# Columns in five chunks of 512 and one of 452, in a Fourier and two-layer kernel

## The chip, the cores and the metric

The kernel runs on one core of a Trainium2 chip. The metric is device time in microseconds (us) of one execution. The kernel before took 933.95 us as the median of three runs (933.7 to 934.25). Beside these, one execution was recorded by the hardware profiler, and every row below is from it.

## The reference

The input `x` has 2 sequences of 3008 rows with 256 values. A two-dimensional Fourier transform is taken of each sequence, and its real part goes through two layers with their own weights.

```
X = np.fft.fft(np.fft.fft(x, axis=1), axis=2)
x = X.real.reshape(6016, 256)                        # float32
h = x @ w_in;  x = (h / (1 + exp(-h))) @ w_out       # 256 -> 2048 -> 256
h = x @ w_in2; g = h * clip(h + 3, 0, 6) / 6
out = g @ w_out2                                      # 6016 x 256
```

The weights are given in a wide (64-bit) format, which the kernel decodes to 32-bit floats itself.

## The kernel before

The Fourier stage writes a tile `eo` (128 partitions, two halves, one column per pair of rows k and -k). There are 2 x 1505 = 3010 such columns (`NPAIR`), and one column stands for two of the 6016 rows: the even and the odd part of the first layer's product, added and subtracted, give both.

All later work goes by chunks of columns, the list `CHUNKS` (line 54). With `CHUNK = 502` there are five chunks of 502 columns and one of 500. A chunk of n columns gives matmuls with n moving columns, and vector instructions of n columns. Tiles with moving data (`x..`, `h`, `ghi`, `glo`) are allocated with 512 columns per half (`LINE`) and used up to n; the staging tiles `st` and `u` and the DRAM buffers follow `CHUNK` or n.

Every 32-bit matrix product is done as three matmuls, helper `mm3` at lines 301 to 303: both operands are split into a high and a low part, and high x high, high x low and low x high are added up in PSUM. Each of these matmuls loads its own 128 x 128 weights.

**First layer** (lines 551 to 660, driven by the loop over `units`). A unit is one chunk and one of 16 blocks of 128 hidden values. `win1` and `win1_end` make the even and the odd product (tile `ab`, 2 x 3 matmuls); VectorE adds the last input row (line 559) and combines them (line 570); `parts` computes the activation on ScalarE; `low` makes the low parts on GpSimd, and for every other unit one of the two on VectorE (line 621); `wout1` makes four products into `y` (4 x 3 matmuls). So a unit has 18 matmuls. The chunks are passed twice: a first pass over 2, 4, 4, 6, 8 and 10 blocks (`PARTS`), a second over the rest. The second pass's result is added to the first's in DRAM by an accumulating store that GpSimd issues (line 663). Beside these units VectorE decodes the weights of both layers; `advance(steps, PACE + ...)` gives the decoder a fixed number of nanoseconds per unit, whatever the width of the chunk.

**Second layer** (the loop over `units2`). A unit is one chunk and two hidden blocks. The 2 x 2 block product is made with seven products instead of eight (tiles `pa`, `pb`, `pc`, `pd`, 7 x 3 matmuls), and `wout2` makes eight products into `y` (8 x 3): 45 matmuls, and 8 units per chunk. The last chunk comes last in both layers' order of chunks.

The order of the work on each engine is written out in the program. SyncE issues the plain transfers; ScalarE issues a few at the start and the end. Dynamic transfers, those of GpSimd, have a scratch area of 16 KB of each SBUF partition, at its start; the program's own tiles lie behind it.

Of the kernel before, what the change touches and what calls it, by code (L numbers as in the profile page):

```python
# [36 lines left out]
F32 = mybir.dt.float32  # L37
# [7 lines left out]
S, D, B = 3008, 256, 2  # L45
NA, NB = 47, 64
NPAIR = B * (S // 2 + 1)
SELF = NB // 2 + 1
HALFB = NPAIR // B
FF, P = 2048, 128  # L50
NF = FF // P
CHUNK = 502
LINE = 512
CHUNKS = [(c, min(CHUNK, NPAIR - c)) for c in range(0, NPAIR, CHUNK)]


NJ = NB // 4
# [24 lines left out]
def body(tc, xh, x128, t1, t2, t3, w1, w128, w2, out):  # L82
    nc = tc.nc
    V, A, T, G = nc.vector, nc.scalar, nc.tensor, nc.gpsimd
# [4 lines left out]
    eop = tc.alloc_tile_pool(name="eop", bufs=1, side="right")  # L89
# [1 line left out]
    w128_sb = per.tile([P, NF], F32, name="w128_sb")  # L91
    consts = per.tile([P, 16], F32, name="consts")
    three, mask, minus, warm = (consts[:, i : i + 1] for i in range(4))
    eo = eop.tile([P, 2, NPAIR], F32, name="eo", tag="eo")
    w2_d = [
        [dr.tile([P, 2, n], F32, name=f"w2{q}_d{g}", tag=f"w2{q}_d{g}") for q, n in (("h", 512), ("l", 512), ("x", 384))]
        for g in range(NF // 2)
    ]
    e128_d = [dr.tile([1, n], F32, name=f"e128_d{j}", tag=f"e128_d{j}") for j, (_, n) in enumerate(CHUNKS)]
    x_d = [[dr.tile([P, 2, n], F32, name=f"x{h}_d{j}", tag=f"x{h}_d{j}") for h in "hl"] for j, (_, n) in enumerate(CHUNKS)]  # L100
    y1_d = [dr.tile([P, 2, 2 * n], F32, name=f"y1_d{j}", tag=f"y1_d{j}") for j, (_, n) in enumerate(CHUNKS)]

# [321 lines left out]
        return c + 256  # L424

    V.memset(three, 3.0)
    G.memset(nil, 0.0)
    cleared = (V, ((2, 0, 1), (2, 2, 3), (3, 0, 2))), (G, ((2, 1, 2), (2, 3, 4), (3, 2, 4), (4, 0, 4), (5, 0, 4)))
    for eng, slots in cleared:
# [17 lines left out]
    i = g = 0  # L447
# [56 lines left out]
    def split_eo(k, j):  # L504
        c, n = CHUNKS[j]
        hi, lo = (xsp.tile([P, 2, LINE], F32R, name=f"x{h}{k}", tag=f"x{2 * (k % 2) + i}") for i, h in enumerate(("hi", "lo")))
        eb = xsp.tile([P, LINE], F32, name=f"eb{k}", tag="eb", bufs=2)
        new = k < len(CHUNKS)
        if new:
            nc.sync.dma_start(e128_d[j], eo[0:1, 1, c : c + n])  # L510
        nc.sync.dma_start(eb[:, :n], e128_d[j].to_broadcast([P, n]))
        if new:
            split(hi[:, :, :n], lo[:, :, :n], eo[:, :, c : c + n], x_d[j])
        else:
            for x, d in zip((hi, lo), x_d[j]):
                nc.sync.dma_start(x[:, :, :n].bitcast(F32), d)
        return hi, lo, eb
# [3 lines left out]
    units = [(k, f) for k, (_, fs) in enumerate(segs) for f in fs]  # L521
    n1 = NF * len(CHUNKS)
    turn = n1 - 10
# [87 lines left out]
    stp = tc.alloc_tile_pool(name="stp", bufs=1, reuse_waits="tile")  # L611
# [15 lines left out]
    def stage_tile(i):  # L627
        return stp.tile([P, 2, 2 * CHUNK], F32, name=f"st{i}", tag=f"st{i}")

# [38 lines left out]
    def moving(k):  # L668

        j = segs2[k][0]
        n = CHUNKS[j][1]
        st = stp.tile([P, 4 * CHUNK + 8], F32, name=f"u{k}", tag="su", bufs=1)
        st = st[:, : 4 * CHUNK].rearrange("p (m c) -> p m c", m=2)
        nc.sync.dma_start(st[:, :, : 2 * n], y1_d[j])
        b11, b12 = st[:, 0, 0:n], st[:, 0, n : 2 * n]
        b21, b22 = st[:, 1, 0:n], st[:, 1, n : 2 * n]
        us[k] = {}

        def high(name, src):
            r = ring[0] % RING
            ring[0] += 1
            x = (xsp if r < NEAR else xq).tile([P, 2, LINE], F32R, name=f"{name}_{k}", tag=f"x{r}")
            us[k][name] = x[:, 0, :n], x[:, 1, :n]
            A.activation(x[:, 0, :n], src, AF.Copy)

        def rest(name, src):
            hi, lo = us[k][name]
            (V if k == 0 and name in ("b21", "t2", "t3") else G).tensor_tensor(out=lo, in0=src, in1=hi, op=ALU.subtract)  # L690

        yield
        high("b11", b11)
        yield
        rest("b11", b11)
        high("b21", b21)
        yield
        rest("b21", b21)
        yield
        V.tensor_tensor(out=b11, in0=b12, in1=b11, op=ALU.subtract)  # L700
        V.tensor_tensor(out=b12, in0=b22, in1=b12, op=ALU.subtract)
        high("t1", b11)
        yield
        rest("t1", b11)
        yield
        V.tensor_tensor(out=b11, in0=b22, in1=b11, op=ALU.subtract)
        V.tensor_tensor(out=b21, in0=b11, in1=b21, op=ALU.subtract)
        high("t2", b11)
        yield
        rest("t2", b11)  # L710
        high("t4", b21)
        yield
        rest("t4", b21)
        high("t3", b12)
        yield
        rest("t3", b12)
        high("b22", b22)
        yield
        rest("b22", b22)
        yield  # L720
# [25 lines left out]
    for i in range(n1):  # L746
        k, f = units[i]
# [34 lines left out]
        if i == n1 - 15:  # L782
            ready = moving(0)
            next(ready)
# [89 lines left out]
    for e, (k, f) in enumerate(units2):  # L874
        j, fs = segs2[k]
        n = CHUNKS[j][1]
        u = us[k]
# [37 lines left out]
        if left == 3 and more:  # L915
            ready = moving(k + 1)
            next(ready)
# [114 lines left out]
def token_columns():  # L1032

    at = {(k % NA, k % NB): k for k in range(S)}
    ks = [at[ka, kb] for ka in range(NA // 2 + 1) for kb in range(NB if ka else SELF)]
    pairs = [(n, k) for n in range(B) for k in ks]
    col = np.zeros(B * S, np.int64)
    for c, n in CHUNKS:
        for i in range(n):
            m, k = pairs[c + i]  # L1040
            col[m * S + (S - k) % S] = 2 * c + n + i
            col[m * S + k] = 2 * c + i
    return col
# [44 lines left out]
```

## Time and profile before

| | |
|---|---|
| median of three runs | 933.95 us (933.7 to 934.25) |
| the profiled execution | 934.05 us, span 932.3 us |
| TensorE busy | 926.3 us (99%), 4286 matmuls |
| VectorE, ScalarE, GpSimd busy | 659.5, 651.8, 530.8 us |
| granted TensorE clock, mean | 0.999 |

The span runs from the first to the last instruction of the profiled execution. A matmul's row has its start and a length; matmuls overlap (the next one starts before the one before has ended), so what counts for the time is the distance between two starts. Weight loads have rows of their own (PEld) and run beside the matmuls. "128x502" in a row is partitions x columns.

### The profile page before, as it was taken

What the parts mean: (1) busy time and instruction counts of PE and PEld (TensorE: products, weight loads), DVE (VectorE), ACT (ScalarE), POOL (GpSimd) and SP (SyncE); (2) the same over time, 40 slices, a digit from 0 to 9 for tenths busy, and PEclk for the clock granted to TensorE, in tenths of its full rate; (3) what the DMA queues carried; (4) which work ended last, traced back from release to release, by engine and by line L of the source; (5) the groups of instructions that cost most, each with busy time, mean ns of one, the idle gap of its engine ahead of it and who ended that gap; (6) DMA issues with size and microseconds to landing.
All of it is one profiled execution on the core that took longest, in us unless ns stands there. A gap on an engine that the chain in (4) does not pass through costs nothing.

```text
span 932.3 us, 12162 instructions
## 1 busy us (share of the span) xinstructions
PE 926.3 (99%) x4286; PEld 775.2 (83%) x4286; DVE 659.5 (71%) x907; ACT 651.8 (70%) x1144; POOL 530.8 (57%) x391
## 2 busy tenths in 40 slices
PE   9999999999999999999999999999999999999998
PEld 8988888888888888888888888888888888888886
DVE  7988898979999999865564565564554555455544
ACT  4878767675767676857776777766776677677665
POOL 2056656654656656534774577755765675576553
PEclk9999999999999999999999999999999999999999
DMA  8554334052273636586130002020020002001001
GB/s 322 196 200 155 135 145 145 1 190 98 101 222 115 200 118 196 176 296 213 63 88 1 1 1 89 0 89 1 1 89 0 1 1 89 1 0 45 1 1 44
DMA packets 27720, 89.27 MB, mean 96 GB/s; under 512 B 2886, under 2 KB 16460, under 8 KB 25132
## 3 DMA queue, kind: packets, MB, share of 16 engines
q1 hardware_dynamic: 26284, 81.81, 24.4%
q0 software_dynamic: 992, 6.16, 3.6%
q8 instruction: 33, 0.54, 0.2%
q10 hardware_dynamic: 384, 0.54, 0.2%
q14 instruction: 27, 0.22, 0.1%
HBM read 52.30 MB, written 36.20 MB: 95 GB/s over the span
## 4 chain that ended last, share of the span: by engine, by line
PE 98%; DMA 0%; DVE 0%; issue 0%; ACT 0%; SPq 0%; DVEq 0%
PE y L301 19%; PE y L302 18%; PE y L303 18%; PE ab L301 5%; PE ab L302 5%; PE ab L303 5%; PE pa L301 4%; PE pa L302 4%; PE pa L303 3%; PE pb L302 2%; PE pb L301 2%; PE pb L303 2%; PE ps L366 1%; PE ps L409 1%; PE pd L302 1%; PE pd L301 1%
## 5 line engine op out<-in xcount | busy, mean ns | idle before, releaser
L805 POOL TENSOR_TENSOR glo<-h,ghi 128x502 fp32r<-128x502 f32 (+1 forms) x191 | 246.6, 1303 | 195.0 <-ACT ghi L802 195.0
L621 POOL TENSOR_TENSOR glo<-h,ghi 128x502 fp32r<-128x502 f32 (+1 forms) x137 | 219.2, 1615 | 188.8 <-ACT h L580 183.1
L301 PE MATMUL y<-ghi,whi 128*128 128x502 f32 (+1 forms) x768 | 298.0, 388 | 0.0
L302 PE MATMUL y<-glo,whi 128*128 128x502 f32 (+1 forms) x768 | 298.0, 388 | 0.0
L303 PE MATMUL y<-ghi,wlo 128*128 128x502 f32 (+1 forms) x768 | 297.8, 388 | 0.0
L303 PEld LDWEIGHTS y<-ghi,wlo 128*128 128x128 f32 x768 | 144.2, 188 | 29.3
L301 PEld LDWEIGHTS y<-ghi,whi 128*128 128x128 f32 x768 | 144.2, 188 | 29.0
L302 PEld LDWEIGHTS y<-glo,whi 128*128 128x128 f32 x768 | 144.2, 188 | 28.9
L802 ACT ACTIVATE ghi<-h 128x502 fp32r<-128x502 f32 (+1 forms) x192 | 118.1, 624 | 47.1 <-DVE h L797 46.8
L579 ACT ACTIVATE ghi<-ab 128x502 fp32r<-128x502 f32 (+1 forms) x96 | 56.5, 588 | 88.5 <-DVE h L570 87.5
L797 DVE SCALAR_TENSOR_TENSOR h<-h,pc 128x502 f32<-128x502 f32 (+1 forms) x96 | 65.1, 678 | 71.7 <-ACT h L794 71.7
L927 DVE TENSOR_TENSOR pc<-u,pb 128x502 f32<-128x502 f32 (+1 forms) x48 | 32.9, 685 | 111.7 <-ACT u L863 111.7
L863 ACT ACTIVATE u<-pa 128x502 f32<-128x502 f32 (+1 forms) x96 | 56.7, 591 | 54.9 <-PE pa L303 52.0
L794 ACT ACTIVATE h<-pc,consts 128x502 f32<-128x502 f32 (+1 forms) x96 | 64.6, 673 | 40.1 <-DVE pc L927 39.0
L559 DVE SCALAR_TENSOR_TENSOR st<-eb,w_sb,ab 128x502 f32<-128x502 f32 (+1 forms) x92 | 67.0, 728 | 19.0 <-PE ab L303 19.0
L301 PE MATMUL ab<-xhi,whi 128*128 128x502 f32 (+1 forms) x192 | 75.2, 392 | 0.1
L302 PE MATMUL ab<-xlo,whi 128*128 128x502 f32 (+1 forms) x192 | 74.7, 389 | 0.0
L303 PE MATMUL ab<-xhi,wlo 128*128 128x502 f32 (+1 forms) x192 | 74.5, 388 | 0.0
L570 DVE SCALAR_TENSOR_TENSOR h<-st,ab 128x502 f32<-128x502 f32 (+1 forms) x92 | 61.4, 668 | 7.0 <-PE ab L303 6.3
L797 DVE SCALAR_TENSOR_TENSOR h<-h,pd 128x502 f32<-128x502 f32 (+1 forms) x96 | 64.5, 671 | 1.2 <-ACT h L794 1.2
L794 ACT ACTIVATE h<-pd,consts 128x502 f32<-128x502 f32 (+1 forms) x96 | 64.7, 674 | 0.6 <-DVE pd L939 0.6
L580 ACT ACTIVATE h<-h 128x502 f32<-128x502 f32 (+1 forms) x96 | 60.0, 625 | 3.0
(165 smaller groups left out, 1572.2 us busy)
## 6 DMA issues: line engine op xcount, KB each, us to landing
raw<-in_w SPq DMA_DIRECT2D x16, 1024.0 KB, 6.9
u<-y_d SPq DMA_DIRECT2D x6, 1004.0 KB, 6.9
y_d<-st SPq DMA_DIRECT2D x5, 1004.0 KB, 4.4
y_d<-st POOLq DMA_DIRECT2D x5, 1004.0 KB, 9.2
out<-st SPq DMA_DIRECT2D x20, 251.0 KB, 2.3
w2h_d<-h SPq DMA_DIRECT2D x8, 512.0 KB, 2.6
w2l_d<-t SPq DMA_DIRECT2D x8, 512.0 KB, 2.6
whi<-w2h_d SPq DMA_DIRECT2D x8, 512.0 KB, 8.9
```

Source lines behind the costliest of these rows:

```text
L301: T.matmul(o, wh, xhi, start=first, stop=False, **group)
L302: T.matmul(o, wh, xlo, start=False, stop=False, **group)
L303: T.matmul(o, wl, xhi, start=False, stop=last, **group)
L559: V.scalar_tensor_tensor(out=z[:, :n], in0=eb[:, :n], scalar=w128_sb[:, f : f + 1], in1=ab[:, :n], op0=ALU.mult, op1=ALU.add)
L570: V.scalar_tensor_tensor(out=h[:, 0, :n], in0=z[:, :n], scalar=2.0, in1=ab[:, :n], op0=ALU.mult, op1=ALU.subtract)
L580: A.activation(h[:, s, :n], src, AF.Silu)
L621: eng.tensor_tensor(out=glo[:, s, :n], in0=h[:, s, :n], in1=ghi[:, s, :n], op=ALU.subtract)
L794: A.activation(h[:, i, :n], c[:, :n], AF.Relu, bias=three)
L797: V.scalar_tensor_tensor(out=h[:, i, :n], in0=h[:, i, :n], scalar=6.0, in1=c[:, :n], op0=ALU.min, op1=ALU.mult)
L802: A.activation(g[0][:, i, :n], h[:, i, :n], AF.Copy)
L805: E.tensor_tensor(out=g[1][:, i, :n], in0=h[:, i, :n], in1=g[0][:, i, :n], op=ALU.subtract)
L863: A.activation(t[:, :n], pa[:, :n], AF.Copy)
```

## The change

`CHUNK` becomes 512 and a new constant `NCOL` = 3012 takes the place of `NPAIR` where columns are counted: there are five chunks of 512 and one of 452. The tile `eo` and the output have two columns more; the two columns of `eo` are set to zero by a memset on VectorE at the start, and on the host they are dropped from the output. The tile `u` loses 8 elements of padding. The scratch for dynamic transfers is set to 8192 bytes of each partition, so that tiles allocated from that side lie 8 KB lower.

```
-CHUNK = 502
+NCOL = 3012
+CHUNK = 512
-CHUNKS = [(c, min(CHUNK, NPAIR - c)) for c in range(0, NPAIR, CHUNK)]
+CHUNKS = [(c, min(CHUNK, NCOL - c)) for c in range(0, NCOL, CHUNK)]
...
-    eo = eop.tile([P, 2, NPAIR], F32, name="eo", tag="eo")
+    eo = eop.tile([P, 2, NCOL], F32, name="eo", tag="eo")
...
     V.memset(three, 3.0)
+    V.memset(eo[:, :, NPAIR:], 0.0)
...
-        st = stp.tile([P, 4 * CHUNK + 8], F32, name=f"u{k}", tag="su", bufs=1)
+        st = stp.tile([P, 4 * CHUNK], F32, name=f"u{k}", tag="su", bufs=1)
...
-        for i in range(n):
+        for i in range(min(n, NPAIR - c)):
...
-    nc = bacc.Bacc("TRN2", target_bir_lowering=False, num_devices=1)
+    nc = bacc.Bacc("TRN2", target_bir_lowering=False, num_devices=1, dynamic_dma_scratch_size=8192)
...
-    out = nc.dram_tensor("out", (P, 2, 2 * NPAIR), F32, kind="ExternalOutput").ap()
+    out = nc.dram_tensor("out", (P, 2, 2 * NCOL), F32, kind="ExternalOutput").ap()
```

## Rows read from the trace of the kernel before

**Rows 1.** The page: busy us (share) and instructions of each engine; the chain's shares.
```profile
PE 926.3 (99%) x4286; PEld 775.2 (83%) x4286; DVE 659.5 (71%) x907; ACT 651.8 (70%) x1144; POOL 530.8 (57%) x391
...
PE 98%; DMA 0%; DVE 0%; issue 0%; ACT 0%; SPq 0%; DVEq 0%
```
**Rows 2.** The chain of waits, its first long piece: start us, us, what.
```profile
1.19 4.26 DMA x<-in_xh
```
**Rows 3.** Groups by shape, PE: line, names, shapes xcount | busy us, mean ns | idle.
```profile
L301 PE MATMUL y<-ghi,whi 128*128 128x502 f32 x640 | 249.0, 389 | 0.0
L301 PE MATMUL ab<-xhi,whi 128*128 128x502 f32 x160 | 62.9, 393 | 0.1
L301 PE MATMUL pa<-t,whi 128*128 128x502 f32 x40 | 15.8, 395 | 0.0
```
**Rows 4.** Timeline of PE, first layer, 502 columns: start us, us, instruction.
```profile
301.47 0.39 PE L301 MATMUL ab<-xhi,whi 128*128 128x502 f32 x1
305.55 0.39 PE L301 MATMUL ab<-xhi,whi 128*128 128x502 f32 x1
```
**Rows 5.** Timeline of PE, first layer, 500 columns.
```profile
159.30 0.38 PE L301 MATMUL ab<-xhi,whi 128*128 128x500 f32 x1
163.26 0.38 PE L301 MATMUL ab<-xhi,whi 128*128 128x500 f32 x1
```
**Rows 6.** Timeline of PE, second layer, 502 columns.
```profile
707.71 0.39 PE L301 MATMUL pb<-b,wx 128*128 128x502 f32 x1
717.92 0.39 PE L301 MATMUL pb<-b,wx 128*128 128x502 f32 x1
```
**Rows 7.** Timeline of PE, second layer, 500 columns.
```profile
870.51 0.39 PE L301 MATMUL pb<-b,wx 128*128 128x500 f32 x1
875.93 0.38 PE L301 MATMUL pd<-t,whi 128*128 128x500 f32 x1
880.55 0.39 PE L301 MATMUL pb<-b,wx 128*128 128x500 f32 x1
```
**Rows 8.** Windows: stretch, its us, busy us (x) by engine, PEclk, DMA share, GB/s.
```profile
150.00:190.00 40.00, 40.00 (x182) 33.95 (x181) 38.55 (x44) 26.23 (x45) 23.60 (x14) 1.00 0.25 84
210.00:390.00 180.00, 179.89 (x793) 148.46 (x792) 174.58 (x206) 121.45 (x212) 105.53 (x67) 1.00 0.46 146
```
**Rows 9.** Groups by shape, VectorE (columns as in Rows 3).
```profile
L559 DVE SCALAR_TENSOR_TENSOR st<-eb,w_sb,ab 128x502 f32<-128x502 f32 x76 | 55.4, 728 | 12.7 <-PE ab L303 12.7
L570 DVE SCALAR_TENSOR_TENSOR h<-st,ab 128x502 f32<-128x502 f32 x76 | 50.8, 668 | 2.7 <-PE ab L303 2.2 <-issue 0.4
L621 DVE TENSOR_TENSOR glo<-h,ghi 128x502 fp32r<-128x502 f32 x44 | 35.9, 815 | 6.2 <-ACT h L580 6.1
L341 DVE TENSOR_TENSOR x<-x 128x512 f32<-128x512 f32 x4 | 2.8, 692 | 0.3
L341 DVE TENSOR_TENSOR x<-x 128x256 f32<-128x256 f32 x5 | 2.1, 426 | 0.2
L426 DVE MEMSET consts<- 128x1 f32 x1 | 0.1, 59 | 0.8 <-PEq L1076 0.8
```
**Rows 10.** The chain of waits, 310 to 330 us (columns as in Rows 2).
```profile
319.38 0.53 issue
319.90 1.63 DVE a L234
```
**Rows 11.** The page, DMA queues: queue, kind: packets, MB, share of 16 engines.
```profile
q0 software_dynamic: 992, 6.16, 3.6%
```
**Rows 12.** Groups by shape, GpSimd (columns as in Rows 3).
```profile
L663 POOL DMA_DIRECT2D y_d<-st x6 | 5.6, 928 | 0.0
```
**Rows 13.** Groups by shape, weight loads (columns as in Rows 3).
```profile
L301 PEld LDWEIGHTS y<-ghi,whi 128*128 128x128 f32 x768 | 144.2, 188 | 29.0
L409 PEld LDWEIGHTS ps<-t_sb,o 128*128 128x128 f32 x96 | 11.7, 192 | 0.4 <-issue 0.2
```
**Rows 14.** The chain of waits in the Fourier stage (columns as in Rows 2).
```profile
20.36 0.89 PE ps L409 x8
```

More of the change, by code (lines that the diff above doesn't have):

```diff
@@ L1085 @@
     y = np.asarray(r.results[0]["out"])
-    y = y.transpose(2, 1, 0).reshape(2 * NPAIR, D)
+    y = y.transpose(2, 1, 0).reshape(2 * NCOL, D)
     return np.ascontiguousarray(y[token_columns()])
```

## The prediction

> **What bounds the kernel now.** I read the page's busy line first: TensorE is busy 926.3 of 932.3 us, with 4286 matmuls, and nothing else is over 71% [rows 1]. The chain of waits comes next: it is TensorE for 98% of it [rows 1], after a first 4.26 us of input [rows 2]. So the time is the number of matmuls times the distance between their starts, and the question of this change is how that distance depends on the number of moving columns. The groups by shape give the counts [rows 3]. Of the three matmuls of each product there is one group each, so 3 x 640 + 3 x 160 + 21 x 40 = 3240 matmuls have 502 columns; the last chunk has 648 with 500, by the same code (16 units of 18 and 8 of 45). The 389 ns in these rows are not the price of one, since matmuls overlap; the distance of the starts is. The timeline gives it over whole units:
> - first layer, 502 columns: 301.47 to 305.55, one unit of 18 matmuls, 4.08 us, 226.7 ns each [rows 4]
> - first layer, 500 columns: 159.30 to 163.26, 3.96 us, 220.0 ns each [rows 5]
> - second layer, 502 columns: 707.71 to 717.92, one unit of 45, 10.21 us, 226.9 ns [rows 6]
> - second layer, 500 columns: 870.51 to 880.55, 10.04 us, 223.1 ns; in it the 24 matmuls up to 875.93 take 225.8 ns, and the 21 after that 220.0 [rows 7]
>
> The granted clock is 1.00 of 2.4 GHz [rows 8], so streaming alone would be 209.2 ns for 502 columns and 208.3 for 500. The surplus is 17.5 ns (42 columns) for 502 and 11.7 ns (28 columns) for 500. Two columns less save 6.7 ns, where streaming explains 0.8. That is the most telling fact of this profile.
>
> **The change part by part.** The number of matmuls, units and instructions stays as it is (six chunks before and after). Moved are the columns: 10 more in 3240 matmuls, 48 fewer in 648, which is 3240 x 10 - 648 x 48 = 1296 columns more, 0.5 us of streaming. By streaming alone the change is worth nothing; all of it lies in the surplus.
>
> No row has 512 or 452 columns. The bounds for 512: 213.3 ns, streaming with no surplus, and 230.8 ns, with the 42 columns of the 502 row. For 452: 188.3 ns at the low end; at the high end 220.0, if something other than the columns set the 500 row. 500, 512 and 452 are multiples of four, 502 is not; I take the nearest row of that kind, 500, and its 28 columns: 540 cycles, **225.0 ns for 512**, and 480 cycles, **200.0 ns for 452**. The step by step sum:
> - first layer, 512: 18 x 225.0 = 4.05 us for 4.08, 80 units: -2.4 us
> - second layer, 512: 45 x 225.0 = 10.125 for 10.21, 40 units: -3.4
> - first layer, 452: 18 x 200.0 = 3.60 for 3.96, 16 units: -5.8
> - second layer, 452: 45 x 200.0 = 9.00 and the 0.14 that today's 10.04 has over 45 x 220.0; 9.14 for 10.04, 8 units: -7.2
>
> This makes -18.8 us, if TensorE stays the bound. Two things take from it, both on VectorE in the first layer, where it decodes weights at a fixed amount per unit beside its two to three instructions on the chunk (lines 559 and 570, and 621 every other unit) [rows 9]. One column costs it (692 - 426) / 256 = 1.04 ns by line 341 [rows 9]. The last chunk's first pass (10 units) runs in the stretch 150 to 190, where VectorE is busy 38.55 of 40 us [rows 8], 3.82 us per unit of 3.96. With 48 columns fewer in 2.5 instructions it needs 3.82 - 0.125 = 3.69 us, over TensorE's 3.60: +0.9 us over 10 units. In 210 to 390 it has 174.58 of 180 us [rows 8], 3.96 per unit of 4.08; with 10 columns more that is 3.98 of 4.05, so its slack shrinks from 0.12 to 0.07 us. There is one visible stall there now, at 319.38, behind a decode step [rows 10]; I count 0.4 us for more like it.
>
> The other parts I cost at nothing. The zeroed two columns are one small memset on VectorE ahead of the memsets of input buffers; it is hidden by the 4.26 us of the first load [rows 2], and without that cover is under 0.1 us (the memset of one column, line 426, takes 59 ns [rows 9]). The smaller scratch concerns the six accumulating stores of GpSimd, 992 packets in all, 0.93 us of issue each [rows 11, 12]; nothing in the trace shows a limit that half the room would reach, GpSimd's products are short of work (57% busy [rows 1]), and they would hide a wait of several us. Were a store to hold GpSimd until the one before has landed, its cost would be bounded by six waits; stores are tens of us apart, so there is nothing to wait for. Transfers grow by 2%, under matmuls.
>
> Sum: -18.8 + 0.9 + 0.4 = -17.5 us. The profiled execution took 934.05 us with a span of 932.3, 0.1 us over the median of 933.95; so the forecast is 933.95 - 17.5 = **916.5 us**.
>
> Could the weight load hold the short chunk back? It lasts 188 ns, starts with the matmul before, and is nearly as long as 452 columns stream [rows 13, 14]. But in the Fourier stage 8 loads and 8 matmuls go by in 0.89 us, 111 ns a pair, with loads of 192 ns [rows 13, 14], so the duration of a load is latency and not its distance to the next. I keep it as a small rival.
>
> **The rivals.**
> (a) *Groups of sixteen, with a whole 512.* Sixteen columns take 6.67 ns at 2.4 GHz, and both distances are whole multiples: 220.0 is 33, 226.7 is 34. If columns are fetched in sixteens and the ragged end of 502 costs a group more than that of 500, a 512 without a ragged end goes in 33 (220.0 ns) and 452 in 30 (200.0). Second layer: 9.90 + 0.14 = 10.04 for 10.21, 40 x 0.17 = -6.8; first layer: 3.96, but VectorE's 3.98 holds the 44 units of 210 to 390, some -0.09 there and -0.12 in 36 others, -8.3; last chunk -13.0 + 0.9. With 0.6 us of stalls: -26.6, **907 us**. For it speaks the exactness of the multiples; against it that 500 and 502 fill the same 32 groups.
> (b) *Groups of sixteen, rounded up after a constant.* (n + 28) rounded up to sixteen: 500 gives 528 cycles, 502 gives 544, exactly the rows; 512 gives 544 too, 226.7 ns, no gain, and 452 gives 480. Then only the short chunk pays: -13.0 + 0.9 + 0.6 = -11.5, **922 us**. For it: one constant explains both rows; against it: 500 then lies exactly on the edge by chance.
> (c) *The surplus is that of a ragged end and goes.* A whole 512 near 213.3 to 218 ns. At 213.3: second layer 9.60 + 0.14 = 9.74, -18.8; first layer 3.84, held at 3.98 in 44 units, -4.4, and -8.6 in the others; last chunk -12.1: -43.9, **890 us**. For it: streaming is all that 512 columns need; against it: no row of four-byte columns shows a surplus so small. The Trainium skill, "TensorE: Matmul & The Clock Gate", section "Wait — 56ns, not 53.3ns?", states such a rule, that back-to-back matmuls start N / 2.4 GHz and about 2.5 ns apart once warm, 215.7 ns for 512; by it the estimate would be 896 us. The trace differs from that rule in all its rows, by 9 ns for 500 columns and 15 for 502.
> (d) *Slower.* 512 keeps the 42 columns of the 502 row: 230.8 ns. First layer 4.155 for 4.08, 80 units: +6.0; second layer 10.39 for 10.21, 40 units: +7.2; 452 at the same surplus, 205.8 ns: -4.1 and -5.1. Together +4.0, **938 us**. It decides from the point where 512 costs 3.7 ns more than 502 does now (230.4 ns: 3240 x 3.7 = 12.1, the gain of the short chunk). For it: the surplus would be one of the long chunk; against it: two fewer columns already take 6.7 ns off.
> (e) *No gain in the short chunk.* The load of the weights sets 220.0 ns for 500 and for 452: with (b) that is no change, **934 us**. Against it the 111 ns in the Fourier stage.
>
> **How the numbers follow.** Forecast 0.30, (a) 0.27, (b) 0.22, (c) 0.11, (d) 0.06, (e) 0.04. Time 916.5 us. From (a) to (b), with some 5 us to either side for the unknown share of second-layer stretches at the slower distance, and part of (c): 893 to 928 us. A measurement of this kernel can tell about 0.2% (1.9 us) from no change. Faster 0.90 (forecast, a, b, c), same 0.04 (e), slower 0.06 (d).
>
> **What would show it.** In the timeline of the changed kernel the starts of first-layer matmuls of 512 columns stand 225.0 ns apart (a unit of 18 in 4.05 us), those of 452 columns 200.0. 220.0 and 4.0 us would be (a), 226.7 and 4.08 (b), 213 to 218 (c), 230.8 (d); 452 at 220 is (e). In the last chunk's first pass VectorE should be without idle time and the unit near 3.7 us, not 3.6. The forecast is wrong if the distance for 512 is one of the rivals', or if the last chunk's second pass takes other than 9.0 to 9.3 us per unit.

## The result and the profile after

The changed kernel took **943.81 us** (943.47 to 944.09, four runs) against 933.9 of before on the same chip: ratio 1.0106, interval 1.0088 to 1.0123. It is 9.9 us slower; 916.5 was forecast, and the range ended at 928. The profiled execution has a span of 941.7 us, 9.4 more than before.

The page says at once where not to look: TensorE is still busy 99% of the span, with the same 4286 matmuls, and the other engines do what they did [rows 1].

```profile
PE 935.3 (99%) x4286; PEld 773.4 (82%) x4286; DVE 662.6 (70%) x908; ACT 651.2 (69%) x1144; POOL 529.9 (56%) x391
```

So each matmul must have become dearer. The timeline of PE over whole units (start us, us, instruction) shows by how much: first layer with 512 columns (two rows, one unit apart), first layer with 452, second layer with 512, second layer with 452.

```profile
301.73 0.39 PE L302 MATMUL ab<-xhi,whi 128*128 128x512 f32 x1
305.93 0.39 PE L302 MATMUL ab<-xhi,whi 128*128 128x512 f32 x1
...
158.41 0.37 PE L302 MATMUL ab<-xhi,whi 128*128 128x452 f32 x1
162.13 0.37 PE L302 MATMUL ab<-xhi,whi 128*128 128x452 f32 x1
...
709.48 0.39 PE L302 MATMUL pb<-b,wx 128*128 128x512 f32 x1
719.96 0.39 PE L302 MATMUL pb<-b,wx 128*128 128x512 f32 x1
...
875.50 0.37 PE L302 MATMUL pb<-b,wx 128*128 128x452 f32 x1
884.74 0.37 PE L302 MATMUL pb<-b,wx 128*128 128x452 f32 x1
```

The first-layer unit of 18 takes 4.20 us with 512 columns, 233.3 ns a matmul; with 502 it took 4.08 [rows 4]. With 452 it takes 3.72 us, 206.7 ns, for 3.96 with 500 [rows 5]. The second-layer unit of 45 takes 10.48 us for 10.21 [rows 6], and 9.24 for 10.04 [rows 7]. Over 80 and 40 units of the long chunks and 16 and 8 of the short one these four differences account for the time: 80 x 0.12 + 40 x 0.27 = 20.4 us more in the long chunks, 16 x 0.24 + 8 x 0.80 = 10.2 us less in the short one; 10.2 us more together, where the span grew by 9.4.

Over streaming (213.3 and 188.3 ns) the surplus is 20.0 ns, 48 columns, for 512, and 18.4 ns, 44 columns, for 452. The prediction had given both the 28 columns of 500.

VectorE, the second mechanism of the prediction, holds nothing here. These are the windows that answer to [rows 8]:

```profile
150.00:190.00 40.00, 40.00 (x191) 35.57 (x190) 38.06 (x45) 27.16 (x49) 24.00 (x16) 1.00 0.25 86
210.00:390.00 180.00, 180.00 (x773) 144.25 (x772) 173.80 (x203) 118.61 (x203) 105.13 (x66) 1.00 0.43 142
```

TensorE is busy in all of both. The stretch 150 to 190 has 191 matmuls, 10.6 units, most of them of 452 columns (from 176 us on some are of 512 again). VectorE needs 38.06 / 10.6 = 3.59 us a unit there, less than TensorE's 40 / 10.6 = 3.77.

### The profile page after: what moved, and what is told of

Same layout as the page of the kernel before. It is cut to its first block, busy times and chain, and to the rows that moved or that the text cites. A ratio compares the mean times of both kernels' runs of the same rounds, so it can differ in the third digit from the quotient of the medians.

```text
span 941.7 us, 12164 instructions
## 1 busy us (share of the span) xinstructions
PE 935.3 (99%) x4286; PEld 773.4 (82%) x4286; DVE 662.6 (70%) x908; ACT 651.2 (69%) x1144; POOL 529.9 (56%) x391
## 4 chain that ended last, share of the span: by engine, by line
PE 98%; ACT 1%; DVE 0%; DMA 0%; issue 0%; SPq 0%; DVEq 0%
PE y L302 18%; PE y L304 18%; PE y L303 18%; PE ab L302 5%; PE ab L303 5%; PE ab L304 5%; PE pa L303 3%; PE pa L302 3%; PE pa L304 3%; PE pb L302 2%; PE pb L304 2%; PE pb L303 2%; PE ps L367 1%; PE pc L302 1%; PE ps L410 1%; PE pd L303 1%
## 5 line engine op out<-in xcount | busy, mean ns | idle before, releaser
L807 POOL TENSOR_TENSOR glo<-h,ghi 128x512 fp32r<-128x512 f32 (+1 forms) x191 | 246.5, 1303 | 196.3 <-ACT ghi L804 192.6
L623 POOL TENSOR_TENSOR glo<-h,ghi 128x512 fp32r<-128x512 f32 (+1 forms) x137 | 216.0, 1593 | 198.3 <-ACT h L582 188.8
L302 PE MATMUL y<-ghi,whi 128*128 128x512 f32 (+1 forms) x768 | 299.5, 390 | 0.0
L304 PE MATMUL y<-ghi,wlo 128*128 128x512 f32 (+1 forms) x768 | 299.5, 390 | 0.0
L303 PE MATMUL y<-glo,whi 128*128 128x512 f32 (+1 forms) x768 | 299.4, 390 | 0.0
L804 ACT ACTIVATE ghi<-h 128x512 fp32r<-128x512 f32 (+1 forms) x192 | 117.9, 624 | 46.8 <-DVE h L799 46.4
L799 DVE SCALAR_TENSOR_TENSOR h<-h,pc 128x512 f32<-128x512 f32 (+1 forms) x96 | 65.0, 677 | 72.6 <-ACT h L796 72.6
L561 DVE SCALAR_TENSOR_TENSOR st<-eb,w_sb,ab 128x512 f32<-128x512 f32 (+1 forms) x92 | 66.9, 727 | 18.2 <-PE ab L304 18.2
L302 PE MATMUL ab<-xhi,whi 128*128 128x512 f32 (+1 forms) x192 | 75.2, 392 | 0.0
L303 PE MATMUL ab<-xlo,whi 128*128 128x512 f32 (+1 forms) x192 | 74.9, 390 | 0.0
L304 PE MATMUL ab<-xhi,wlo 128*128 128x512 f32 (+1 forms) x192 | 74.8, 390 | 0.0
```

What stands on the lines that cost most here:

```text
L302: T.matmul(o, wh, xhi, start=first, stop=False, **group)
L303: T.matmul(o, wh, xlo, start=False, stop=False, **group)
L304: T.matmul(o, wl, xhi, start=False, stop=last, **group)
L561: V.scalar_tensor_tensor(out=z[:, :n], in0=eb[:, :n], scalar=w128_sb[:, f : f + 1], in1=ab[:, :n], op0=ALU.mult, op1=ALU.add)
L623: eng.tensor_tensor(out=glo[:, s, :n], in0=h[:, s, :n], in1=ghi[:, s, :n], op=ALU.subtract)
L799: V.scalar_tensor_tensor(out=h[:, i, :n], in0=h[:, i, :n], scalar=6.0, in1=c[:, :n], op0=ALU.min, op1=ALU.mult)
```

## The experiments

In all of them a "start" is the first byte of a tile in its partition, modulo 256. The edit of a1 is against the kernel before, all others are against the changed kernel. Runs for which no ratio is given have one execution each. Before and after, the first layer's moving tiles start at 192 and the weights at 0. Before, the second layer's own moving tiles start at 64 or 192 (after, 0 or 192), and its weights `wx` at 192.

**a1: the scratch alone.**

The kernel before with one edit:

```
-    nc = bacc.Bacc("TRN2", target_bir_lowering=False, num_devices=1)
+    nc = bacc.Bacc("TRN2", target_bir_lowering=False, num_devices=1, dynamic_dma_scratch_size=8192)
```

> The kernel before (502 and 500 columns) with only the scratch for dynamic transfers cut to 8 KB, so that weights and the left-hand tiles lie 8 KB lower. Theory A (the width: a matmul's distance follows from its number of columns): nothing changes, 226.7 ns for 502, 220.0 for 500, 934 us. Theory B (where the moving tiles start, relative to 256 bytes): the same, since those starts are kept. Theory C (the 8 KB shift makes weight loads and moving reads collide, which would be why 452 came at 206.7 and not 200.0): 502 rises by a group of 6.67 ns to 233.3 in much of the kernel, 500 to 226.7, time 945 us or more.

It took 934.06 us, ratio 0.9999 (0.9989 to 1.0009); the unit with 502 columns takes 4.08 us, as before:

```profile
302.03 0.39 PE L301 MATMUL ab<-xhi,whi 128*128 128x502 f32 x1
306.11 0.39 PE L301 MATMUL ab<-xhi,whi 128*128 128x502 f32 x1
```

Theory C falls: neither the smaller scratch nor the move by 8 KB costs anything. The loss lies in the other edits: the widths, with the tiles where they are.

**a2: 512 columns at another start.**

```
-            flat = eop.tile([P, NF * 384 + 8], F32R, name="wx", tag="eo")[:, : NF * 384]
+            flat = eop.tile([P, NF * 384 + 8 + 48], F32R, name="wx", tag="eo")[:, : NF * 384]
```

> The changed kernel (512 and 452) with the right-hand tiles, among them all moving tiles of the first layer, moved 192 bytes down, to starts that are whole multiples of 256 bytes (they start at 192 above one now). Theory A: 512 stays at 233.3 ns, 944 us. Theory B: 512 columns are 2048 bytes and from an aligned start touch no line more than they fill; the distance falls by at least one group of 6.67 ns, to 226.7 or less, and the time by 3000 matmuls x 6.67 ns = 20 us or more, to 924 us or less.

The 192 bytes move `wx` and all tiles below it, so that moving tiles and weights of both layers start at 0. It took 927.75 us, ratio 0.9932 (0.9918 to 0.9947): faster than before, and 16.1 us faster than the changed kernel. The unit takes 4.08 us, 226.7 ns a matmul, where it took 4.20:

```profile
301.60 0.39 PE L302 MATMUL ab<-xhi,whi 128*128 128x512 f32 x1
305.68 0.39 PE L302 MATMUL ab<-xhi,whi 128*128 128x512 f32 x1
```

So the same matmul with the same 512 columns costs 6.7 ns more or less in these units (6.0 on the mean of the first layer, 233.3 and 227.3) by where its tiles start, and that decides whether this change wins or loses. 452 stayed at 206.3 ns on average.

**a3, a4, b4: many widths in one kernel.** The six chunks get different widths, so that one run reads six distances. This is a3; a4 has (510, 506, 502, 498, 490, 504), and b4 is a3 with the 48 elements of a2.

```
+SIZES = (512, 508, 504, 500, 496, 492)
...
-CHUNKS = [(c, min(CHUNK, NCOL - c)) for c in range(0, NCOL, CHUNK)]
+CHUNKS = [(sum(SIZES[:j]), n) for j, n in enumerate(SIZES)]
```

> The changed kernel with chunks of 512, 508, 504, 500, 496 and 492 columns (3012 in all), starts of tiles as in the changed kernel. One look gives the distance for each width in the first layer. Theory A with rounding up to sixteen columns after a constant: a staircase, 233.3 for 512, and 500 at 220.0 as before; 504 and 508 on 226.7, 496 and 492 on 213.3 or 220.0. If the ragged end matters (the width's remainder to sixteen), 496, a whole multiple like 512, stands out from its neighbours: at or above 500, as 512 is above 502. Theory C: 500 does not come at 220.0 here but at 226.7.

> The changed kernel with chunks of 510, 506, 502, 498, 490 and 504 columns (3010). Theory A with a staircase: 510 and 506 at 226.7 or 233.3, 502 at 226.7, 498 and 490 at 220.0 or 213.3, monotone together with the widths of the run beside it. If widths that are not multiples of four cost extra, 498 lies above 500 (226.7 or more) and 490 above 492. Theory C: 502 at 233.3.

> Chunks of 512, 508, 504, 500, 496 and 492 columns at aligned starts. At 192 the same widths came at 233, 229, 229, 220, 220 and 220 ns. Theory D: each one group of 6.67 ns less (226.7, 222, 222, 213, 213, 213), time some 20 us under 934. Theory E: only 512 falls, to 226.7, the others stay; 931 us.

They took 933.73 us (a3), 939.09 (a4) and 931.15 (b4). Mean distances in the first layer, in ns:

```
width            490    492    496    498    500    502    504    506    508    510    512
start 192       220.2  220.1  220.1  226.6  220.8  226.8  228.7  230.4  229.4  227.2  233.1
start 0 (b4)           220.7  221.8         223.6         227.1         227.6         227.6
```

This is no staircase: 510 comes cheaper than 504, 506 and 508, and 498 dearer than 500. At start 0 the widths behave otherwise, 512 falls and 500 rises; that speaks against theory D, by which all should fall, and only partly for E. 500 at start 192 is one of the cheapest of all, relative to its width.

**b1: the old widths at start 0**, with the 48 elements of a2.

```
+SIZES = (502, 502, 502, 502, 502, 500)
```

> The widths of before (five of 502, one of 500; scratch 8 KB, staging tiles as wide as after) with all moving tiles at starts that are multiples of 256 bytes. Theory D (an aligned start takes one group of 6.67 ns off whatever the width): 502 at 220.0 and 500 at 213.3 ns, some 22 us less, 912 us. Theory E (only where the end falls matters: a tile that starts at 192 spills 64 bytes less than its length over the last 256-byte line, so 512 gains from alignment and 502 does not): 226.7 and 220.0 as before, 934 us.

It took 931.09 us, ratio 0.9965 (0.995 to 0.9979), between the two theories. 502 fell to a mean of 223.9 ns over both layers (the unit below takes 4.03 us); 500 rose to 225.5 in the first layer, from the 220.0 of [rows 5].

```profile
301.89 0.39 PE L303 MATMUL ab<-xhi,whi 128*128 128x502 f32 x1
305.92 0.38 PE L303 MATMUL ab<-xhi,whi 128*128 128x502 f32 x1
```

**b2, b3: the starts 128 and 64** (16 and 32 elements instead of 48).

> The changed kernel (512, 452) with the right-hand tiles at 128 above a multiple of 256 bytes. If what counts is a multiple of 128 bytes: as at a multiple of 256, 512 at 226.7 ns, 928 us. If it is 256: 512 at 233.3, 944 us.

> The changed kernel with the right-hand tiles at 64 above a multiple of 256 bytes. If starts that are odd multiples of 64 are all alike: as at 192, 512 at 233.3 ns and 944 us. If the distance grows with the spill into the last line, it lies at another value than 233.3; 226.7 or less would mean that 192 alone is bad.

b2 took 941.89 us, ratio 1.0082 (1.0067 to 1.0097), with first-layer means of 233.1 ns for 512; b3 935.71 us, with 229.0 ns. So 512 has four prices in the first layer: 227.3 at start 0, 229.0 at 64, 233.1 at 128, 233.3 at 192.

**c1, c2: the start of the weights.** The weight tiles of group g start at 64 x (g modulo 4); c1 has moving tiles at 0, c2 at 192.

```
+        at = 16 * (g % 4)
...
+            t = wp.tile([P, 1088], F32R, name=f"w{q}{key}_{g}", tag=f"w{q}{g}")
+            d[key, g] = t[:, at : at + 1024].rearrange("p (i c) -> p i c", i=2)
```

> The aligned changed kernel (512 and 452, moving tiles at whole multiples of 256 bytes) with the weight tiles of the eight groups of hidden blocks starting 0, 64, 128 and 192 bytes above such a multiple, in turn, so that one run has four starts of weights. Theory F (the load of the next weights and the moving read get in each other's way, and what counts is where one starts relative to the other): 512 stays at 226.7 ns in groups 0 and 4 and changes in the others, to 233.3 in some. Theory G (only the moving tile's start counts): 226.7 in all groups.

> The changed kernel (moving tiles at 192) with the same four starts of the weight tiles. Theory F: 512 falls from 233.3 to 226.7 ns in groups 3 and 7, where weights start at 192 too. Theory G: 233.3 in all groups.

They took 937.43 and 938.71 us. First-layer means for 512, in ns, by the start of the weights of the second of the two matmuls:

```
weights at           0      64     128     192
moving at 0 (c1)    229.2  233.1  232.9  230.0
moving at 192 (c2)  233.1  232.8  229.9  229.3
```

Read along the difference (moving minus weights, modulo 256) the two lines are one: 0 gives 229.2 and 229.3, 64 gives 230.0 and 229.9, 128 gives 232.9 and 232.8, 192 gives 233.1 and 233.1. Theory G falls, theory F's relative start stands. The 229.2 of the difference 0 is over a2's 227.3 because matmuls of several groups alternate here: where four matmuls before and four after have the same starts, the mean is 227.8 in c1 and 227.6 in c2. In c2's timeline nine matmuls of one group with weights at 192 take 2.04 us, and of one with weights at 0 2.10:

```profile
246.18 0.39 PE L304 MATMUL y<-ghi,whi 128*128 128x512 f32 x1
248.22 0.39 PE L304 MATMUL y<-ghi,whi 128*128 128x512 f32 x1
...
267.59 0.39 PE L304 MATMUL y<-ghi,whi 128*128 128x512 f32 x1
269.69 0.40 PE L304 MATMUL y<-ghi,whi 128*128 128x512 f32 x1
```

**e1: narrower loads.**

```
-                mm3(y[2 * m + s][:, :n], wh, wl, hi[:, s, :n], lo[:, s, :n], first, last)
+                c = P if first else (64, 32)[m]
+                mm3(y[2 * m + s][:c, :n], wh[:, :c], wl[:, :c], hi[:, s, :n], lo[:, s, :n], first, last, skip_group_check=True)
```

> The changed kernel with narrower weights in the first layer's second products, in all hidden blocks of a pass but the first: 64 of the 128 weight columns for one half of the outputs and 32 for the other (the rest of these products is left out); the products into ab keep 128. Moving columns stay at 512 and 452. Theory F (the load of the next weights reads beside the moving data and takes time from it): the surplus over streaming falls with the width of the load that runs beside a matmul: 512 at 233.3 ns beside a load of 128 columns, about 223 beside 64 and 218 beside 32; 452 at 206.7, 197 and 193. Theory H (the surplus belongs to the moving read itself or to the change from one matmul to the next): 233.3 and 206.7 beside every load.

This kernel leaves out the rest of those products. The loads did become shorter (groups by shape, weight loads: mean ns of one is the number before the last bar):

```profile
L302 PEld LDWEIGHTS y<-ghi,whi 128*128 128x128 f32 x432 | 81.0, 188 | 17.6
L302 PEld LDWEIGHTS y<-ghi,whi 128*64 128x64 f32 x168 | 22.6, 134 | 11.3
L302 PEld LDWEIGHTS y<-ghi,whi 128*32 128x32 f32 x168 | 18.3, 109 | 17.9
```

The matmuls hardly followed. Six with loads of 128 columns, six of 64 and six of 32 take 1.40, 1.39 and 1.39 us in this stretch:

```profile
312.87 0.39 PE L302 MATMUL ab<-xhi,whi 128*128 128x512 f32 x1
314.27 0.40 PE L302 MATMUL y<-ghi,whi 128*64 128x512 f32 x1
315.66 0.40 PE L302 MATMUL y<-ghi,whi 128*32 128x512 f32 x1
317.05 0.40 PE L302 MATMUL ab<-xhi,whi 128*128 128x512 f32 x1
```

On average 233.1, 232.6 and 232.4 ns; 452 columns 205.9, 205.5 and 203.8. So theory F holds in its place (the relative start) and falls in its cause: the surplus does not shrink with the load, where F expected 10 to 15 ns less and 0.4 to 2.1 were measured. H's distances are close to what was measured, but H does not say why the weights' start matters. The kernel took 942.5 us. It has no relative start but 192 in the first layer, so nothing is shown for the others.

**f1, f2: eleven widths against eight starts.** Weights of group g start at 32 x g; widths (512, 508, 504, 500, 496, 492) and (510, 506, 502, 498, 494, 500).

> Six widths (512, 508, 504, 500, 496, 492) against eight starts of the weights, 32 bytes apart, group by group; moving tiles at 192 above a multiple of 256 bytes. If width and relative start set the distance together, each width has its own good and bad starts: 512 is at 227 to 230 ns with weights at 128 to 192 and at 233 with weights at 0 and 64, as before, and 500 is at 220 with weights at 0 and at 224 to 226 with weights at 192. If the mean over the starts is what a width costs, the means grow with the width by 0.42 ns per column, at a surplus of some 16 ns over streaming. If starts that are odd multiples of 32 bytes are worse, every width is slower in the odd groups.

> The same eight starts of the weights with 510, 506, 502, 498, 494 and 500 columns. 502 at 226.7 ns with weights at 0 and 223 to 224 with weights at 192; the means over the starts on the same line as those of the run beside it, so that widths that are not multiples of four cost nothing extra. If they do cost extra, the means of 510, 506, 502, 498 and 494 lie above that line by 2 ns or more.

The means of the distance in ns, by moving minus weights, for matmuls of both layers whose neighbours have the same starts (distances over 250 ns, waits, left out; 452 from the six kernels that have it at the four starts). The last column is the mean over all starts (eight, four for 452) in columns of 0.417 ns, less the width.

```
width      0      64     128     192   mean of all starts  surplus
452      206.4   205.4  206.6   206.4   206.2              42.9
492      221.3   222.6  221.8   221.1   222.6              42.3
494      223.2   224.5  226.9   220.7   223.6              42.7
496      223.0   226.5  224.7   222.5   224.5              42.7
498      226.9   226.6  226.9   226.6   227.1              47.1
500      225.8   226.4  226.7   221.1   225.7              41.8
502      226.0   227.3  227.3   226.6   228.4              46.1
504      227.5   229.0  233.3   229.5   229.4              46.5
506      228.2   229.7  228.1   230.1   230.6              47.4
508      228.2   229.9  228.8   229.3   229.9              43.8
510      228.0   230.1  233.0   226.9   230.6              43.5
512      229.2   230.2  233.6   233.1   232.5              45.9
```

Taken over its starts, every width costs its streaming and 42 to 47 columns more, 17.4 to 19.8 ns. Multiples of four have 42 to 47, the others 43 to 47. Around the mean each width has its own good and bad starts. 500 at 192 is 4.6 ns under its mean, the farthest under it in this table; 512 at 192 is on the dear side. Odd multiples of 32 bytes were not worse throughout: 500 costs 223.8 at a difference of 160 and 227.6 at 96. The two runs took 939.71 and 940.56 us.

One cell that the table leaves out is dearer than all in it. 502 columns at a difference of 96 came at 236 ns on average in f2, and not evenly: at 225 to 233 ns in some matmuls and at 243 to 250 in others, as here, where the starts are 0.22 and 0.25 us apart:

```profile
301.03 0.39 PE L305 MATMUL ab<-xhi,whi 128*128 128x502 f32 x1
301.25 0.42 PE L306 MATMUL ab<-xlo,whi 128*128 128x502 f32 x1
301.50 0.41 PE L307 MATMUL ab<-xhi,wlo 128*128 128x502 f32 x1
```

So width and relative start do not fix a price to the nanosecond. 502 at a difference of 0 also came at 223.9 ns in b1 and at 226.0 here.

**d1, d2: the version that follows.** Five chunks of 500 and one of 510, in their cheap cells at 192 (the tile `u` gets 48 elements more, so that the second layer's moving tiles start there too). d2 also puts `wx` at 0 and takes work from VectorE; the second edit is d2's.

```
+SIZES = (500, 500, 500, 500, 500, 510)
...
-        for s, eng in ((1, G), (0, V if shared or f % 2 else G)):
+        for s, eng in ((1, G), (0, V if shared or f % 4 == 1 else G)):
```

> Five chunks of 500 and one of 510 columns (3010, no zeros), all moving tiles at 192 above a multiple of 256 bytes, the start at which 500 came at 220.8 ns and 510 at 227.2 in the runs so far; scratch 8 KB. If the distance belongs to the width and the start as read there, five widths at 220.8 and one at 227.2 against five at 226.8 and one at 222.0: 648 x (5 x 6.0 - 5.2) = 16 us less than before, 918 us; second-layer stretches at the slower distance may take 3 us of it. If the 500 chunk was quick only as the last chunk (smaller weights traffic, other engines less loaded), 500 comes at 226 and the time is 934 us.

> The version with five chunks of 500 and one of 510, with two edits more: GpSimd takes half of VectorE's low parts in the first layer (line 623, one unit in four instead of one in two), and the second layer's weights wx start at a whole multiple of 256 bytes, like the other weights. If VectorE bounds parts of the first layer there (162.2 of 165 us busy, TensorE 161.9), TensorE's idle time of some 3 us in 210 to 375 goes; and if the relative start sets the distance, second-layer matmuls beside wx fall from 223.2 to 220.4 ns, 45 x 8 x 5 units with 9 of 45 such loads: 0.9 us. Together 921 us for 924.7. If the stalls come from the decode's own order and not from VectorE's load, 924.

d1 took **924.68 us**, ratio 0.9898 (0.9881 to 0.9914), d2 **923.13 us**, ratio 0.9881 (0.9864 to 0.9897): 1.2% faster than before and 2.2% faster than the changed kernel. In d1 a first-layer unit takes 3.96 us, the 220.0 ns that were expected:

```profile
300.16 0.38 PE L303 MATMUL ab<-xhi,whi 128*128 128x500 f32 x1
304.12 0.38 PE L303 MATMUL ab<-xhi,whi 128*128 128x500 f32 x1
```

In d2 the second layer's mean for 500 fell from 221.0 ns (223.2 beside `wx`) to 220.1, so the relative start works there as well. But 918 us was not reached, and d2's other edit missed. The windows of d1 (the first row) and of d2 (the second; columns as in [rows 8]) show why: TensorE now has idle time in the first layer, and it kept it in d2.

```profile
210.00:375.00 165.00, 161.92 (x724) 134.62 (x723) 162.20 (x188) 110.37 (x192) 98.37 (x62) 1.00 0.46 148
```
```profile
210.00:375.00 165.00, 160.91 (x724) 134.88 (x723) 160.28 (x178) 110.58 (x193) 109.18 (x72) 1.00 0.48 148
```

VectorE's load fell by 1.9 us, TensorE's idle time grew from 3.1 to 4.1. The ten low parts that went to GpSimd (line 623) are 8.3 us of VectorE's time, but other steps took longer, line 132 by 2.5 us. The rows are groups by shape in 210 to 375, two of d1 and the same two of d2:

```profile
L623 DVE TENSOR_TENSOR glo<-h,ghi 128x500 fp32r<-128x500 f32 x20 | 16.5, 823 | 1.8 <-ACT h L582 1.8
L132 DVE TENSOR_SCALAR t<-a 128x1024 int32<-128x1024 int32 x8 | 10.8, 1356 | 0.1
...
L623 DVE TENSOR_TENSOR glo<-h,ghi 128x500 fp32r<-128x500 f32 x10 | 8.2, 819 | 2.3 <-ACT h L582 2.3
L132 DVE TENSOR_SCALAR t<-a 128x1024 int32<-128x1024 int32 x8 | 13.3, 1663 | 0.1
```

So d2 hardly took load from VectorE, and it does not tell whether VectorE's sum of work holds the faster matmuls. The chain of waits in d1 shows one of the stalls, at the place where before had its one [rows 10]:

```profile
317.05 1.62 issue
318.67 1.62 DVE a L236
320.30 0.58 DVE h L572
320.88 0.66 DVE st L561
```

The chain calls its first piece `issue`, but VectorE does not stand still there. Its timeline has one long row of line 235 over that piece (the first row below is the same step of line 236 elsewhere, for comparison):

```profile
228.57 0.55 DVE L236 TENSOR_TENSOR a<-a 128x384 fp32r<-128x384 f32 x1
...
316.46 2.29 DVE L235 TENSOR_TENSOR t<-t,h 128x1024 fp32r<-128x1024 f32 x1
318.67 1.62 DVE L236 TENSOR_TENSOR a<-a 128x384 fp32r<-128x384 f32 x1
```

Two decode steps in a row hold VectorE for 3.83 us, nearly a whole unit of 3.96, and the two steps that the matmul waits for stand behind them. The program counts 1.7 us for the two (`yield 1700`). So at this place the decode's place and length in VectorE's order hold the matmul. The other stalls were not followed, and what makes the same step last 0.55 or 1.62 us was not tried.

## Why the prediction was wrong

**Right:** that the time is the number of matmuls times the distance of their starts; that all of the change lies in the surplus over streaming; the counts; that the scratch costs nothing (a1; memset and transfers were not tried alone, but the four distances leave nothing for them); that the weight load's 188 ns do not hold the short chunk at 220 ns, rival (e) (452 came at 206.7). The price of the changed kernel follows from the measured distances alone.

**The step that failed:** "500, 512 and 452 are multiples of four, 502 is not; I take the nearest row of that kind, 500, and its 28 columns". Both halves failed. Multiples of four are no kind of their own (f1, f2: 42 to 47 columns against 43 to 47). And 500's 28 columns were the exception, not the rule: a cheap cell at the relative start of 192, where the same width costs 224 to 228 ns at other starts (f1, f2). The ordinary surplus is 42 to 47 columns, and the 42 of the 502 row, which the prediction set aside as that of a ragged end, was the ordinary row. 512 fell on one of its dear cells (48), 452 on an ordinary one (44). The mis-sized terms are -2.4 and -3.4 us for the long chunks, measured +9.6 and +10.8, and -5.8 and -7.2 for the short one, measured -3.8 and -6.4.

**The rivals.** (d) had the right side and the right mechanism, 512 with 502's surplus, at a chance of 0.06; even its 938 us was short, by 5.8 us, since 512 at this start has 48 columns and not 42. Its point of decision held: 512 cost 6.6 ns more than 502 did, over the 3.7 that it named. (a), (b) and (c) are refuted as rules: the exact multiples of 6.67 ns are also in the new rows (233.3 is 35, 206.7 is 31), but they do not follow from the width: 452 takes 31 and not 30, 498 and 502 take 34 where 500 takes 33, and 512 takes 34 or 35 by its start. The rule of the Trainium skill, "TensorE: Matmul & The Clock Gate", section "Wait — 56ns, not 53.3ns?", a surplus of about 2.5 ns, is met nowhere here: the smallest is 11.7 ns.

**What should have warned.** Inside the rows of before, 500 itself has two prices: 220.0 and 225.8 ns in one unit [rows 7]. The prediction carried the difference as 0.14 us for "stretches at the slower distance" and did not ask what it meant: that the width alone does not set the price, and that 220.0 might be the lucky one. With the mean surplus of the four units [rows 4 to 7], 15.4 ns for any width, 512 comes at 228.7 ns and 452 at 203.7: 3240 x 1.9 - 648 x 18.0 = 5.5 us less, a third of the forecast, with both signs in reach of one unlucky start.

**VectorE.** The two terms, +0.9 and +0.4 us, were not seen in the changed kernel, because its matmuls were slower than forecast. In d1 and d2 TensorE is idle for 3 to 4 us in 210 to 375, more than the 0.4 us counted there. The stall that was followed lies behind decode steps, as that term said; d2 does not settle whether VectorE's sum of work, the ground of the 0.9, has a part in it.

## What to carry to other kernels

A price read from one width and one placement of tiles is one cell, not a law: before a tile's width is changed, the distance of matmul starts is read at several widths and several starts, which one kernel with uneven chunks gives in one run. Where TensorE is busy 99%, the start of moving tiles relative to the weights is worth as much as the width (16 us here, for 48 elements of padding). And when matmuls get quicker, look at once at the place in the other engines' order where a stall already shows.

## What was not expected of the hardware

- With 32-bit data and new weights for every matmul, the starts of two matmuls stand streaming plus 11.7 ns (500 columns at 192, a unit of before) to 23.3 ns (504 at 128) apart, with one cell at 27 (502 at 96). Over all relative starts it is 17.4 to 19.8 ns for the widths measured between 452 and 512.
- The distance depends on the start of the moving tile minus that of the weights (modulo 256 bytes was read): 512 columns at 227.3 ns (0), 229.0 (64), 233.1 (128), 233.3 (192), means of first layers that keep one difference throughout.
- It hardly depends on the length of the weight load, for 512 columns at 192: 233.1, 232.6 and 232.4 ns beside loads of 188, 135 and 108 ns.
- What makes the surplus, and why many steady stretches come in whole multiples of sixteen columns (206.7, 220.0, 226.7, 233.3 ns), stays open.
